# Threshold attention and Fourier mixing on one core: the last 64 queries' scores as four 64x64 tiles, the transform's rest as row tiles

## The chip, the cores and the metric

The kernel runs on one core of a Trainium2 chip. The metric is device time in microseconds (us) for one execution; the number that counts is the median of several. In the profile PE is TensorE's matmuls and PEld its weight loads, DVE is VectorE, ACT is ScalarE, POOL is GpSimd, and SP is the queue on SyncE that issues nearly all transfers. All data is fp32, and one fp32 matmul stands in the trace as two passes.

## The reference

```python
def _attn_ref(q, k, v, tau):            # (8, 8, 576, 64) each: batch, head, row, dim
    scores = np.matmul(q, k.transpose(0, 1, 3, 2)) / 8
    thresh = np.max(scores, axis=-1, keepdims=True) - tau
    scores = np.where(scores >= thresh, scores, -1e9)
    attn = np.exp(scores - np.max(scores, axis=-1, keepdims=True))
    return np.matmul(attn / (np.sum(attn, axis=-1, keepdims=True) + 1e-9), v)

def _moe_ref(x, w_ch1, w_ch2):          # x: the heads side by side, (8, 576, 512)
    u = x + np.real(np.fft.fft(np.fft.fft(x, axis=1), axis=2))
    un = (u - mean(u)) / np.sqrt(var(u) + 1e-6)          # over the last axis
    return u + np.maximum(un @ w_ch1, 0) @ w_ch2         # 512 -> 2048 -> 512
```

## The kernel before, in words

There are 8 batches of 4 pairs of heads. A pair has 576 queries and 576 keys per head, and its attention takes five steps (t = 0 to 4): four of 128 queries for both heads, and a fifth for the last 64 queries of both heads. So there are 160 steps, 20 to a batch. The program is written out by hand in one order for all engines (`manual_schedule`): each engine does its own instructions in that order, and waits on semaphores where it needs another's result.

A step does the following.

- `scores(i)` multiplies queries by keys into one or two score tiles of PSUM (tag "sc", two buffers of two banks). In steps 0 to 3 (L440) head 0 lies on partitions 0 to 63 and head 1 on 64 to 127 of `qT` and `kT`, and each head has its own tile: 288 keys in one bank and 288 in the other, so four matmuls with 64 rows. In step 4 (L446) both heads share a tile of 128 queries: `q_ends` holds the 64 queries of each head on the diagonal of a 128x128 block with zeros beside it, so one matmul over all 128 rows gives each query its own head's scores. Two matmuls of 288 keys.
- The softmax: VectorE takes the negated maxima (L461 in the first two batches, L520 later), ScalarE the exponentials (L469, L526) and the threshold `thr` (L473, L530), VectorE the mask times the exponentials with the sums beside it (L477, L540), and then the inverse of the sum (L385, L388). The mask is the last reader of the score tile. In the first two batches `softmax` does all of it; later it is cut in `softmax_first`, `softmax_second` and `softmax_third` (the scaling of the weights on ScalarE, L549), with other work between.
- `weights_in_parts(i - 1)` transposes the weights of the step before on TensorE (L587 for the last keys, L605 for the rest) and ScalarE copies them to SBUF (L593, L597, L607, L609). `values_in_parts` multiplies them by v (L636) twice per pair.
- `prep_pair(n + 1)` transposes q and k of the next pair on VectorE (L408 and L409 for `kT`, L411 for `qT`), in step 3 of each pair; `load_pair(n + 2)` and `load_v(n + 1)` issue transfers on SP.

After the last pair of a batch, `mixing(b)` does the Fourier transform as a generator, a part at a time: `py` (L766) along the 512 channels for the folded rows in three row blocks u = 0, 1, 2 of 128, 48 and 128 rows, each with an even and an odd half; then `over_seq` (L783, L787) along the 576 rows: for each of two tiles of 128 channels a sine sum `pb` and a cosine sum `pa`, of 289 outputs each. Each takes four matmuls: the main rows for even and for odd outputs (`seq_even`, `seq_odd`, 128 rows each) and the remaining rows (`seq_xe`, `seq_xo`: up to 48 rows of a 128-row matmul, mostly zeros). Sums and differences of `pa` and `pb` then go to the residual stream on VectorE and GpSimd.

The two large products run on groups of 512 tokens, the first group plainly (L909, L933), the others with block products built from sums of blocks (L1210 for ph, L1400 for po), whose results VectorE takes out of PSUM (L1147, L1420). From the second batch on `fill` puts pieces of this work and of `mixing` between the parts of the steps, by a count of TensorE columns (`per_slot`); `fill(True)` takes no part of the mixing. In the first batch `busy` puts dummy matmuls (pd) there. The tiles of PSUM for all but the scores share four banks (tag "mm").

Of the kernel before, what the change touches and what calls it, by code (L numbers as in the profile page):

```python
# [47 lines left out]
def kernel(  # L48
# [12 lines left out]
    nc = tc.nc  # L61
# [81 lines left out]
    def load_v(n):  # L143

        b, p = n // NPAIR, PAIRS[n % NPAIR]
        vt = v_in[n % 2]
        for j in range(2):
            h = 2 * p + (j + p) % 2
            nc.sync.dma_start(
                out=vt[:, j:8:2, :], in_=v[b, h, 0:512, :].rearrange("(t p) d -> p t d", p=128)  # L150
            )
            nc.sync.dma_start(out=vt[64 * j : 64 * j + 64, 8 + j, :], in_=v[b, h, 512:576, :])
# [12 lines left out]
    for u in range(2):  # L165
        for j in range(2):
            nc.gpsimd.memset(v_in[u][64 - 64 * j : 128 - 64 * j, 8 + j, :], 0.0)


    q_ends = const.tile([128, 128], FP32, name="q_ends")  # L170
    nc.gpsimd.memset(q_ends[:, :], 0.0)
# [29 lines left out]
    seq_xe = const.tile([128, 2, NE], FP32, name="seq_xe")  # L201
    seq_xo = const.tile([128, 2, NO], FP32, name="seq_xo")


    SEQ = (
        (((0, 1, 128),), seq_even, 0, ((0, 128),)),
        (((0, 16, 128),), seq_odd, 1, ((0, 128),)),
        (((0, 129, 16), (16, 0, 1)), seq_xe, 0, ((0, 17),)),
        (((32, 0, 16),), seq_xo, 1, ((32, 16),)),
    )  # L210

    def load_seq():
        for u, (pieces, dst, parity, parts) in enumerate(SEQ):
            for p, r, n in pieces:
                nc.sync.dma_start(out=f[p : p + n, u, 0 : 2 * KH], in_=dft_seq[r : r + n, :])
            if dst is seq_xo:
                nc.sync.dma_start(out=f[32:33, u, KH : 2 * KH], in_=dft_seq[144:145, KH : 2 * KH])

    def copy_seq():
        nc.gpsimd.memset(seq_xe[:, :, :], 0.0)  # L220
        nc.gpsimd.memset(seq_xo[:, :, :], 0.0)
        for u, (pieces, dst, parity, parts) in enumerate(SEQ):
            for p, n in parts:
                for c in range(2):
                    nc.gpsimd.tensor_copy(
                        dst[p : p + n, c, :], f[p : p + n, u, KH * c + parity : KH * (c + 1) : 2]
                    )
# [155 lines left out]
    def inverse(i, nh):  # L383
        den = sb.tile([128, 2], FP32, tag="den", bufs=3, name="den")
        nc.vector.tensor_reduce(  # L385
            out=den[:, 0:nh], in_=den_eps[i % 3][:, 0:nh, :], axis=AXIS_X, op=ALU.add
        )
        nc.vector.reciprocal(den[:, 0:nh], den[:, 0:nh])  # L388
# [3 lines left out]
    steps = {}  # L392
# [1517 lines left out]
```

## Time and profile before

| | |
|---|---|
| Median of three runs | 1544.85 us (1543.75, 1544.85, 1545.0) |
| The profiled execution | 1547.94 us; span from first to last instruction 1546.2 us |
| Granted TensorE clock | 0.997 |
| Fifth step's scores (L446) | 128 passes, 36.3 us busy, 406 ns each |
| Other steps' scores (L440) | 1024 passes, 168.4 us busy, 430 ns each |
| Transform along the rows (L783, L787) | 320 passes, about 287 ns each |
| Transform along the channels (L766) | 240 passes |

The length of one matmul instruction includes its way through the array, and the next begins meanwhile: the time that it takes from TensorE is the distance between starts. Batches 0 and 1 (40 steps) run to 275 us, batches 2 to 6 take 168 to 188 us each, batch 7's last step begins at 1302 us, and the rest is the last transform and the last groups' products.

### The profile page before, as it was taken

To read this page: it belongs to the slowest core of one execution; us is meant where nothing else is said; L and a number is where in the kernel's file an instruction comes from. 1 tells how busy PE (TensorE), PEld (TensorE's weight loads), DVE (VectorE), ACT (ScalarE), POOL (GpSimd) and SP (SyncE) were. 2 spreads that over 40 slices of the span, in tenths; PEclk is the share of its full clock that TensorE was granted. 3 is DMA by queue.
4 is the path that set the end of the run, shared out by engine and by line. 5 is a ranking of instruction groups with operands and counts; after the bars stand their busy time and mean duration, and the time that the engine had idled before them with its cause. 6 is when DMAs were issued, how large, how long until landed. Compare 5 with 4: busy or idle time off the path is not lost.

```text
span 1546.2 us, 27021 instructions
## 1 busy us (share of the span) xinstructions
PE 1524.0 (99%) x9786; PEld 1186.0 (77%) x9786; DVE 1063.2 (69%) x2141; ACT 916.4 (59%) x1921; POOL 779.4 (50%) x964
## 2 busy tenths in 40 slices
PE   9999999999999999999999999999999999999999
PEld 5556555556788778887788878887788778989999
DVE  7977676846779466866578566956687657746546
ACT  6875676655666576656775666666665676133131
POOL 3775563034365642546255724554264625647635
PEclk9999999999999999999999999999999999999999
DMA  7423233465956354644455354635464534646655
GB/s 171 130 59 119 78 92 105 139 183 165 280 187 206 92 173 125 186 113 146 146 167 160 120 159 133 199 92 172 120 195 132 160 117 142 220 163 231 234 196 184
DMA packets 248907, 239.31 MB, mean 155 GB/s; under 512 B 197027, under 2 KB 218533, under 8 KB 228678
## 3 DMA queue, kind: packets, MB, share of 16 engines
q1 hardware_dynamic: 246262, 237.28, 50.1%
q8 instruction: 78, 1.28, 0.3%
q10 hardware_dynamic: 2512, 0.30, 0.1%
q14 instruction: 55, 0.45, 0.1%
HBM read 205.93 MB, written 31.46 MB: 154 GB/s over the span
## 4 chain that ended last, share of the span: by engine, by line
PE 91%; DVE 4%; ACT 2%; POOL 1%; DMA 1%; issue 0%; ACTq 0%; DVEq 0%; POOLq 0%
PE ph L1210 25%; PE po L1400 21%; PE pv L636 10%; PE sc L440 10%; PE pw L605 7%; PE po L933 4%; PE ph L909 3%; PE sc L446 2%; PE py L766 2%; PE pe L587 1%; PE pa L783 1%; PE pn L858 1%; PE pa L787 1%; PE pm L360 1%; PE po L1379 1%; DVE neg L461 1%
## 5 line engine op out<-in xcount | busy, mean ns | idle before, releaser
L520 DVE TENSOR_REDUCE neg<-sc 128x1 f32<-128x576 f32 x216 | 154.3, 751 | 117.1 <-PE sc L440 105.5
L526 ACT ACTIVATE e<-sc,neg 128x576 f32<-128x576 f32 x216 | 158.6, 734 | 114.3 <-DVE neg L520 114.3
L1147 DVE TENSOR_TENSOR hs<-ph,hs 128x512 f32<-128x512 f32 (+1 forms) x128 | 105.3, 823 | 167.1 <-PE ph L1210 97.3
L1400 PE MATMUL po<-w,w_all 128*128 128x128 f32 x1728 | 219.4, 276 | 0.0
L1400 PEld LDWEIGHTS po<-w,w_all 128*128 128x128 f32 x1728 | 205.4, 192 | 7.4 <-issue 4.0
L1156 POOL TENSOR_TENSOR w<-hs 128x512 f32<-128x512 f32 x32 | 42.1, 1317 | 312.3 <-ACT hs L1152 249.3
L540 DVE SCALAR_TENSOR_TENSOR e<-sc,thr,e 128x576 f32<-128x576 f32 x216 | 168.4, 812 | 27.2 <-ACT thr L530 27.1
L1210 PE MATMUL ph<-u_t,w 128*128 128x256 f32 x768 | 180.9, 382 | 0.6 <-DMA w<-f 0.6
L607 ACT COPY e_t<-pw 128x512 f32<-128x512 f32 x256 | 148.4, 594 | 44.2 <-PE pw L605 42.7
L440 PE MATMUL sc<-kT,qT 64*128 64x288 f32 x1024 | 168.4, 430 | 5.9 <-DVE e L477 5.5
L605 PE MATMUL pw<-ident,e 128*128 128x128 f32 x1152 | 169.3, 274 | 3.7 <-ACT ends L593 1.9
L549 ACT ACTIVATE e<-e,den 128x576 f32<-128x576 f32 x216 | 157.4, 774 | 2.9 <-DVE den L388 2.2
L1210 PEld LDWEIGHTS ph<-u_t,w 128*128 128x128 f32 x768 | 140.9, 190 | 23.6 <-issue 5.3
L1210 PE MATMUL ph<-w_all,w 128*128 128x256 f32 x672 | 157.1, 382 | 1.1 <-DVE w_all L1132 1.0
L605 PEld LDWEIGHTS pw<-ident,e 128*128 128x128 f32 x1152 | 135.8, 141 | 19.3 <-issue 5.6
L1263 POOL TENSOR_TENSOR w_all<-w_all 128x128 f32<-128x128 f32 (+2 forms) x160 | 121.7, 777 | 44.5 <-DVE w_all L1420 23.4
L1210 PEld LDWEIGHTS ph<-w_all,w 128*128 128x128 f32 x672 | 123.5, 190 | 23.9 <-issue 4.9
L1152 ACT ACTIVATE hs<-hs 128x512 f32<-128x512 f32 (+1 forms) x96 | 74.1, 772 | 113.8 <-DVE hs L1147 113.0
L440 PEld LDWEIGHTS sc<-kT,qT 64*128 64x128 f32 x1024 | 95.1, 186 | 55.4 <-issue 22.9
L1400 PE MATMUL po<-w,hs 128*128 128x128 f32 x912 | 119.8, 278 | 0.0
L1400 PEld LDWEIGHTS po<-w,hs 128*128 128x128 f32 x912 | 109.8, 192 | 9.5 <-issue 8.0
L636 PE MATMUL pv<-e_t,v_in 128*64 128x320 f32 (+1 forms) x512 | 72.1, 423 | 1.5 <-ACT e_t L609 0.8
(227 smaller groups left out, 2910.6 us busy)
## 6 DMA issues: line engine op xcount, KB each, us to landing
w<-f SPq DMA_DIRECT2D x150, 1024.0 KB, 4.9
hs<-in_moe_w_ch_dram SPq DMA_DIRECT2D x23, 512.0 KB, 4.7
q_in<-in_q_dram SPq DMA_DIRECT2D x128, 72.0 KB, 4.1
out_dram<-u SPq DMA_DIRECT2D x36, 256.0 KB, 2.5
k_in<-in_k_dram SPq DMA_DIRECT2D x124, 72.0 KB, 2.4
v_in<-in_v_dram SPq DMA_DIRECT2D x64, 128.0 KB, 5.1
f<-w SPq DMA_DIRECT2D x14, 512.0 KB, 3.3
f<-w SPq DMA_DIRECT2D x7, 1024.0 KB, 4.8
```

What stands on the lines that cost most here:

```text
L440: nc.tensor.matmul(sc[j][:, c, 0:HALF], qT[hp, 128 * t : 128 * t + 128], kT[hp, k0 + HALF * c : k0 + HALF * (c + 1)], start=True, stop=True,)
L520: nc.vector.tensor_reduce(out=neg[:, j : j + 1], in_=sc[j][:, :, 0:HALF], axis=AXIS_XY, op=ALU.max, negate=True,)
L526: nc.scalar.activation(out=ej, in_=sc[j][:, :, 0:HALF], func=ACT.Exp, bias=neg[:, j : j + 1], scale=1.0)
L540: nc.vector.scalar_tensor_tensor(out=ej, in0=sc[j][:, :, 0:HALF], scalar=thr[:, j : j + 1], in1=ej, op0=ALU.is_ge, op1=ALU.mult, accum_out ...
L549: nc.scalar.activation(out=e[:, S * j : S * (j + 1)], in_=e[:, S * j : S * (j + 1)], func=ACT.Copy, scale=den[:, j : j + 1],)
L605: nc.tensor.transpose(pw[:, c, :], e[:, c0 : c0 + 128], ident[:, :])
L607: nc.scalar.copy(e_t[:, 4 * j : 4 * j + 4, qs], pw[:, :, :])
L636: nc.tensor.matmul(pv[64 * j : 64 * j + 64, 0:m], vt[:, 2 * c + j, :], e_t[:, 4 * j + c, 0:m] if c < 4 else ends[:, 0, 0:m], start=(c == 0 ...
L1147: nc.vector.tensor_tensor(out=to, in0=bank, in1=to if other is None else other, op=ALU.add)
L1210: nc.tensor.matmul(bank[:, 256 * q : 256 * q + 256].rearrange("p (two n) -> p two n", two=2), left[:, 256 * c + 128 * q : 256 * c + 128 * ...
L1263: return lambda: eng.tensor_tensor(out=to, in0=to, in1=other, op=ALU.add)
L1400: nc.tensor.matmul(to, lefts[m][j][:, s], right_[:, 128 * s : 128 * (s + 1)], start=jn in (0, 4) and s == 0, stop=s == 3, skip_group_check ...
```

## The change

- The fifth step's scores become four matmuls with 64 rows and 64 columns: head j gives the rows, half c of the keys gives the columns, so that partition 64c + q of the tile holds query q with half c of the keys of both heads. `q_ends` is a plain 128x64 copy. A query's maximum and sum are then on two partitions, and `exchange` brings the halves together with two small reductions on VectorE, once for the maxima and once for the sums. The exponentials, masks and scalings of that step go by head: two of 128x288 for one of 128x576. In the transposed weights four copies of 32 partitions bring the last keys together.
- In the other steps a head's 576 scores lie side by side in PSUM, split over the banks as 256 and 320 keys (head 0) and 320 and 256 (head 1). The keys are in another order: `kT` holds keys 256 to 575, then 0 to 319, with 32 more between, from four transposes for two; v is loaded to fit, with three transfers a head for two.
- In the transform, the remaining rows of the sine (partitions 64 to 127) and of the cosine (0 to 63) become one 64-row matmul of 289 outputs each, issued side by side ahead of the main ones (`rest_of_seq`). For the sine's rows to stand there, the odd half of block u = 1 is made with 128 columns. The points at which the generator stops move: one stop behind sine and cosine together, and two empty ones.
- From batch 2 on, `prep_pair` for the second pair of a batch is called in that batch's fifth step behind `softmax_first`, no longer at the end of its fourth.

```diff
+        for p, n, parity, c in ((0, 17, 0, 0), (32, 16, 1, 0), (64, 17, 0, 1), (96, 16, 1, 1)):
+            nc.gpsimd.tensor_copy(
+                seq_x[p : p + n, parity:KH:2],
+                f[p : p + n, 2, KH * c + parity : KH * (c + 1) : 2],
+            )
...
@@ -380,16 +379,23 @@
     for den in den_eps:
         nc.vector.memset(den[:, :, :], 1e-9)
 
-    def inverse(i, nh):
+    den_ends = const.tile([128, 2, 3], FP32, name="den_ends")
+    nc.vector.memset(den_ends[:, :, :], 1e-9)
+    own = const.tile([128, 2, 2], FP32, name="own")
+
+    def inverse(i):
         den = sb.tile([128, 2], FP32, tag="den", bufs=3, name="den")
-        nc.vector.tensor_reduce(
-            out=den[:, 0:nh], in_=den_eps[i % 3][:, 0:nh, :], axis=AXIS_X, op=ALU.add
-        )
-        nc.vector.reciprocal(den[:, 0:nh], den[:, 0:nh])
+        parts = den_eps[i % 3]
+        if i % NT == 4:
+            parts = den_ends
+            exchange(parts[:, :, 2], parts[:, :, 0:1])
+        nc.vector.tensor_reduce(out=den[:, :], in_=parts[:, :, :], axis=AXIS_X, op=ALU.add)
+        nc.vector.reciprocal(den[:, :], den[:, :])
         return den
 
     heads = {}
     steps = {}
...
@@ -404,9 +410,12 @@
 
 
         q_raw, k_raw = loaded.pop(n)
-        kT = sb.tile([128, D + S], FP32, tag="kT", name="kT")
-        nc.vector.transpose(kT[:, D : D + S], k_raw[:, :])
-        nc.vector.transpose(kT[64:128, 0:D], k_raw[64:128, 512:S])
+        kT = sb.tile([128, S + 96], FP32, tag="kT", name="kT")
+        nc.vector.transpose(kT[:, 0:320], k_raw[:, 256:S])
+        nc.vector.transpose(kT[:, 352:672], k_raw[:, 0:320])
+        for j, k0 in ((0, 288), (1, 256)):
+            hp = slice(64 * j, 64 * j + 64)
+            nc.vector.transpose(kT[hp, 320:352], k_raw[hp, k0 : k0 + 32])
         qT = sb.tile([128, S], FP32, tag="qT", bufs=1, name="qT")
         nc.vector.transpose(qT[:, :], q_raw[:, :])
...
-        sc = [ps.tile([128, 2, 512], FP32, tag="sc", name=f"sc{j}") for j in range(nh)]
+        sc = [
+            ps.tile([128, 2, 512], FP32, tag="sc", name=f"sc{j}") for j in range(2 if t < 4 else 1)
+        ]
+        order = [(c, j) for c in range(2) for j in range(2)]
+        if i < per_batch and t < 4:
+            order.sort(key=lambda cj: cj[1])
+        for c, j in order:
+            hp = slice(64 * j, 64 * j + 64)
+            if t < 4:
+                k0, k1 = ((64, 320), (352, 672), (0, 320), (352, 608))[2 * j + c]
+                to = sc[j][:, c, 512 - (k1 - k0) : 512] if c == 0 else sc[j][:, c, 0 : k1 - k0]
+                left = qT[hp, 128 * t : 128 * t + 128]
+            else:
+                k0, k1 = ((64, 352), (352, 640), (32, 320), (320, 608))[2 * j + c]
+                to, left = sc[0][64 * c : 64 * c + 64, j, 0:HALF], q_ends[hp, :]
+            nc.tensor.matmul(
+                to, left, kT[hp, k0:k1], start=True, stop=True, skip_group_check=t == 4
+            )
         if t < 4:
-            order = [(c, j) for c in range(2) for j in range(2)]
-            if i < per_batch:
-                order.sort(key=lambda cj: cj[1])
-            for c, j in order:
-                if True:
-                    hp, k0 = slice(64 * j, 64 * j + 64), D * (1 - j)
-                    nc.tensor.matmul(
-                        sc[j][:, c, 0:HALF], qT[hp, 128 * t : 128 * t + 128],
-                        kT[hp, k0 + HALF * c : k0 + HALF * (c + 1)], start=True, stop=True,
-                    )
+            steps[i] = [
+                sc[j][:, :, :].rearrange("p c n -> p (c n)")[:, 256 - 64 * j : 832 - 64 * j]
+                for j in range(2)
+            ]
         else:
-            for c in range(2):
-                nc.tensor.matmul(
-                    sc[0][:, c, 0:HALF], q_ends[:, :], kT[:, D + HALF * c : D + HALF * (c + 1)],
-                    start=True, stop=True,
+            steps[i] = [sc[0][:, j, 0:HALF] for j in range(2)]
+
...
+        both = bass.AP(
+            tensor=sc[0].tensor, offset=sc[0].offset,
+            ap=[list(sc[0].ap[0]), [512, 2], list(sc[0].ap[1])],
+        )
+        nc.vector.tensor_reduce(
+            out=own[:, :, 0], in_=both, axis=AXIS_X, op=ALU.max, negate=True
+        )
+        exchange(own[:, :, 1], own[:, :, 0:1])
+        nc.vector.tensor_reduce(out=neg[:, :], in_=own[:, :, :], axis=AXIS_X, op=ALU.min)
+        return neg
+
+    def exchange(out_, in_):
+
+        for half in range(2):
+            a, b = 64 * half, 64 - 64 * half
+            nc.vector.tensor_reduce(
+                out=out_[a : a + 64], in_=in_[b : b + 64], axis=AXIS_X, op=ALU.min
+            )
...
+        if i % NT == 4:
+            exponentials(i, e, neg, thr, 0)
+        for j in range(2):
+            if i % NT < 4:
+                exponentials(i, e, neg, thr, j)
+            elif j == 0:
+                exponentials(i, e, neg, thr, 1)
+            masked(i, e, thr, j)
             if between is not None and j == 0:
                 next(between)
...
+        c0 = 512 if t < 4 else 256
...
@@ -593,22 +618,30 @@
             nc.scalar.copy(ends[:, 0:kept, q0 : q0 + 128], pe[:, 0:kept, :])
         else:
             for j in range(2):
-                hp = slice(64 * j, 64 * j + 64)
-                nc.scalar.copy(ends[hp, 0:kept, q0 : q0 + 64], pe[hp, 0:kept, hp])
+                for half in range(2):
+                    p0 = 64 * j + 32 * (1 - half)
+                    nc.scalar.copy(
+                        ends[p0 : p0 + 32, 0, q0 : q0 + 64],
+                        pe[32 * j : 32 * j + 32, 0, 64 * half : 64 * half + 64],
+                    )
+            if kept == 2:
+                nc.scalar.copy(ends[:, 1, q0 : q0 + 64], pe[:, 1, 0:64])
...
@@ -762,43 +795,47 @@
             for odd in range(2):
                 py = ps.tile([128, 512], FP32, tag="mm", bufs=4, name="py")
                 table, first = (dim_s, 0) if odd else (dim_c, 1)
+                p0 = 64 if u == 1 and odd else 0
+                m, rows = p0 + n if p0 == 0 else 128, slice(p0, p0 + n)
                 for c, c0, c1 in SIN if odd else COS:
                     nc.tensor.matmul(
-                        py[0:n, c0:c1], f[:, c, odd * FW + r : odd * FW + r + n],
+                        py[0:m, c0:c1], f[:, c, odd * FW + r - p0 : odd * FW + r - p0 + m],
                         table[:, c0:c1], start=True, stop=True, skip_group_check=True,
                     )
                 y = y_o if odd else y_e
                 nc.scalar.copy(
-                    y[0:n, u, 0:256].rearrange("p (g hi lo) -> p lo hi g", hi=2, lo=2),
-                    py[0:n, first : first + 256].rearrange("p (lo hi g) -> p lo hi g", lo=2, hi=2),
+                    y[rows, u, 0:256].rearrange("p (g hi lo) -> p lo hi g", hi=2, lo=2),
+                    py[rows, first : first + 256].rearrange("p (lo hi g) -> p lo hi g", lo=2, hi=2),
...
-        def over_seq(y, odd, cols, m):
+        def rest_of_seq(y, rows, cols, m):
             pa = ps.tile([128, 512], FP32, tag="mm", bufs=4, name="pa")
-            for parity, u, table, extra in ((0, 0, seq_even, seq_xe), (1, 2, seq_odd, seq_xo)):
-                at = pa[0:m, parity:KH:2]
+            nc.tensor.matmul(
+                pa[0:m, 0:KH], y[rows, 1, cols], seq_x[rows, :], start=True, stop=False,
+                skip_group_check=True,
+            )
+            return pa
+
+        def over_seq(pa, y, odd, cols, m):
+            for parity, u, table in ((0, 0, seq_even), (1, 2, seq_odd)):
                 nc.tensor.matmul(
-                    at, y[:, u, cols], table[:, odd, :], start=True, stop=False,
-                    skip_group_check=True,
+                    pa[0:m, parity:KH:2], y[:, u, cols], table[:, odd, :], start=False,
+                    stop=True, skip_group_check=True,
                 )
-                nc.tensor.matmul(
-                    at, y[:, 1, cols], extra[:, odd, :], start=False, stop=True,
-                    skip_group_check=True,
-                )
-            return pa
 
         settle(b)
         for t in range(2):
             cols = slice(128 * t, 128 * t + 128)
             tmp = sb.tile([128, 3, KH], FP32, tag="tmp", bufs=1, name="tmp")
             low, high, sin = (tmp[:, c, :] for c in range(3))
-            pb = over_seq(y_o, 1, cols, 128)
+            pb = rest_of_seq(y_o, slice(64, 128), cols, 128)
+            pa = rest_of_seq(y_e, slice(0, 64), cols, 128)
+            over_seq(pb, y_o, 1, cols, 128)
             nc.scalar.copy(sin, pb[:, 0:KH])
-            yield MIX / 11
-            pa = over_seq(y_e, 0, cols, 128)
+            over_seq(pa, y_e, 0, cols, 128)
 
             nc.vector.tensor_tensor(out=low, in0=pa[:, 0:KH], in1=sin, op=ALU.subtract)
             nc.vector.tensor_tensor(out=high, in0=pa[:, 0:KH], in1=sin, op=ALU.add)
@@ -819,10 +856,14 @@
             add(3 - t, every, high, low)
             if t == 1:
                 add(3, slice(0, 1), high[0:1, :], low[0:1, :])
-            yield MIX / 11
+            yield 2 * MIX / 11
+            if t == 0:
+                yield 0
+                yield 0
...
@@ -1764,6 +1805,8 @@
             next(values, None)
         if i < total:
             softmax_first(i)
+        if i % per_batch == 4:
+            prep_pair(n + 1)
         next(values, None)
         if i % per_batch == 3:
             mix(1)
@@ -1806,7 +1849,7 @@
                 prep_ends(n)
             if t == 2 and n + 1 < B * NPAIR:
                 scale_q(n + 1)
-            if t == 3 and n + 1 < B * NPAIR:
+            if t == 3 and n + 1 < B * NPAIR and n % NPAIR:
                 prep_pair(n + 1)
         if wanted:
             wanted.pop().factors()
```

## The prediction, made before the result was known

> **What bounds the kernel now.** I read the page's busy times and chain first, then TensorE's waits, then the timeline around the edited bursts.
>
> ```profile
> PE 1524.0 (99%) x9786; PEld 1186.0 (77%) x9786; DVE 1063.2 (69%) x2141; ACT 916.4 (59%) x1921; POOL 779.4 (50%) x964
> ...
> PE 91%; DVE 4%; ACT 2%; POOL 1%; DMA 1%; issue 0%; ACTq 0%; DVEq 0%; POOLq 0%
> ```
>
> ```profile
> PE sc L440 <- DVE e L477: 5.5, 7, 1.2
> PE ph L1210 <- DVE hs L1147: 2.1, 5, 0.8
> ```
>
> TensorE is busy 99% of the span and idle for 22 us; its longest wait, scores behind a mask (L477, batches 0 and 1 only), is 5.5 us in all. So a nanosecond less of matmul is a nanosecond less of time, except where VectorE decides. But a busy row is not a price: matmuls overlap, so I price by starts, here from TensorE's timeline (start, length, form, number of passes; one fp32 matmul is two passes).
>
> ```profile
> 838.62 1.14 PE L446 MATMUL sc<-kT,q_ends 128*128 128x288 f32 x4
> 839.59 1.05 PE L1400 MATMUL po<-w,hs 128*128 128x128 f32 x8
> 840.48 1.06 PE L1400 MATMUL po<-w,w_all 128*128 128x128 f32 x8
> 841.47 0.64 PE L766 MATMUL py<-dim_s,f 128*48 128x128 f32 x4
> 842.03 0.33 PE L587 MATMUL pe<-ident,e 128*128 128x128 f32 x1
> 842.20 0.60 PE L605 MATMUL pw<-ident,e 128*128 128x128 f32 x4
> ...
> 898.22 2.38 PE L636 MATMUL pv<-e_t,v_rev 128*64 128x320 f32 x16
> 900.42 0.71 PE L636 MATMUL pv<-ends,v_rev 128*64 128x320 f32 x4
> 901.07 0.33 PE L587 MATMUL pe<-ident,e 128*128 128x128 f32 x1
> ...
> 903.83 1.89 PE L1210 MATMUL ph<-u_t,w 128*128 128x256 f32 x8
> 905.65 1.24 PE L440 MATMUL sc<-kT,qT 64*128 64x288 f32 x8
> 906.83 1.99 PE L1210 MATMUL ph<-u_t,w 128*128 128x256 f32 x8
> 908.65 0.27 PE L587 MATMUL pe<-ident,e 128*128 128x128 f32 x1
> ```
>
> The old fifth step takes 838.62 to 839.59, 0.97 us for 4 passes, 243 ns each, with no gap on either side. The 64-row bursts (L440) put 8 passes into 1.18 us: they run in twos, 4 slots of 243 ns, so row tiles do overlap. But they pay at the edges. Eight ph passes alone take 1.73 us (216 ns each); before the burst they take 1.82 (+0.09), after it 1.82 (+0.09), and the burst itself is 0.21 over its 0.97. A visit to 64-row tiles therefore costs about 0.40 us.
>
> **The skill.** "TensorEngine Tiling (Array Packing)", section Tiling Modes (Key Properties), says that changing the tile shape drains TensorE while tiles of one shape run independently. The rows agree and give the price: 0.40 us around L440. The same page's Tile-to-Partition Mapping lists the four 64x64 tiles; no row of this trace has them. "TensorE: Matmul & The Clock Gate", Part 3, says that row and column packing compose, at about 4 ns per further tile; here row tiles (L440) and 64-column tiles (pv, 10 slots of 0.27 us in 2.85) each overlap by two, which supports it without showing four. I go by the trace's prices, and by the page only for four at once.
>
> **The change, part by part.**
>
> 1. Fifth step's scores, 32 pairs. Old 0.97 us. New: four 64x64 matmuls, 8 passes; four at once they fill 2 slots, 0.485 us. Edges: in 0.09, out 0.09 and 0.10 as for L440; inside, the first slot of 64-column pv shows 0.05 (2.20 us for 8 slots of 0.269), not the 0.10 of L440; issue 0.02. Sum 0.845, saving 0.125 us. It counts where TensorE decides: 24 pairs of batches 2 to 7 and three early ones, 27 x 0.125 = 3.4. Bounds: if two column tiles in a row take turns, 4 slots and 1.33 us, so +0.36 per pair; at best, half the edges hidden, saving 0.3.
> 2. Transform over the sequence, 8 batches x 2 column tiles. Old: 16 passes of 0.123 (pa rows: 8 in 0.99), 1.97 us, no edges. New: both rests side by side as row tiles, 2 slots of 0.243, edges 0.40, then 8 passes, 0.985: 1.87. Saves 0.10 x 16 = 1.6; between 0 (edges 0.1 dearer) and 3.
> 3. Odd half of the middle 48 rows now 128 columns wide. The row at 841.47 is such a visit to narrow tiles: 0.10 more on the po passes ahead (0.99 for 0.89), 0.12 in it (0.56 for four of 0.111), 0.06 behind (0.17 for 0.11). 0.28 saved in the six transforms where it stands alone; in the first and the last it follows the even half, which stays narrow, and saves nothing: 6 x 0.28 = 1.7, between 0 and 2.3.
> 4. Scores of the other four steps: 256 and 320 keys for 288 and 288. Each row tile still streams 576, and in batch 0 the second head's first pass starts 13 ns after the first head's though four passes stand ahead of it in program order, so the tiles queue apart: 0. If they went in lockstep, 4 slots of 0.27 for 0.243, 0.11 x 128 = 14 us; I find that unlikely.
> 5. The moved yields put each column tile's cosine matmuls straight behind its sine, with no pe and pw between. Today the first cosine pa waits behind pw (512.57 to 512.86, 0.29 us), about once in each late batch. I count four of six as won, -1.0; from +1 (two banks held at once make pw wait instead) to -1.7.
> 6. VectorE gets longer in every fifth step. The rows:
>
> ```profile
> L385 DVE TENSOR_REDUCE den<-den_eps 128x2 f32<-128x4 f32 x128 | 20.1, 157 | 4.4
> L408 DVE STREAM_TRANSPOSE kT<-k_in 128x576 f32<-128x576 f32 x32 | 24.8, 774 | 3.9 <-DMA k_in<-in_k_dram 3.8
> L409 DVE STREAM_TRANSPOSE kT<-k_in 64x64 f32<-64x64 f32 x32 | 7.8, 242 | 0.4
> ```
>
> (mean ns behind the comma.) Transposes: 774 for 576 and 242 for 64 make 1.04 ns an element, so 508 for 320 and 209 for 32; two of each, 1434 for 1016: +0.42. Maxima: three small reductions of 157: +0.47. Mask: 812 + 82 becomes twice 512 + 82: +0.29. Denominator: two more reductions: +0.31. Together 1.5 us a pair, 1.2 of it ahead of the release of the score bank. In batches 2 to 7 that hides: VectorE works 4.6 of the 7.74 us of the step at 838.62. In batches 0 and 1 it doesn't always, as VectorE (first two rows) and TensorE there show:
>
> ```profile
> 63.26 0.81 DVE L477 SCALAR_TENSOR_TENSOR e<-sc,thr,e 128x576 f32<-128x576 f32 x1
> 63.99 0.08 DVE L477 DVE_READ_ACCUMULATOR e<-sc,thr,e 128x1 f32 x1
> ```
> ```profile
> 63.39 1.98 PE L440 MATMUL sc<-kT,qT 64*128 64x288 f32 x8
> 65.30 1.98 PE L360 MATMUL pm<-w,ones 128*128 128x512 f32 x4
> ```
>
> The next scores take 1.91 us, not 1.18: their second head waits for the mask's end at 64.08. Every ns there is paid, and behind it queue pm, the transposes and all later TensorE work. The same is so after the fifth steps at 118.07 (scores 2.02 long) and 199.11 (1.92). The one at 31.39 has its mask end just as the next scores start, but TensorE then idles 1.08 us at 39.0 anyway: 0.4 left. The other four have 1 us or more of slack. At the very start the transposes stand ahead of the first scores: 0.42. Sum: 3 x 1.2 + 0.4 + 0.42 = 4.4, and 0.3 for ScalarE's three extra copies of the ends in batch 0: 4.7. Bounds: 0.4, if only the start shows; 8 x 1.3 + 0.4 = 10.8, if all show.
> 7. prep_pair of a batch's second pair moves from the end of step 4 to behind the maxima of step 5. Now its transposes run till 839.22 and the maxima wait for VectorE until 840.40, though the scores are done at 839.76. Afterwards the maxima come first, then 2.2 us of transposes, and behind them the po sum at L1420 (841.07 now, about 843 then) which empties a bank for the second group of pw, 843.59 now. I count 0; if the bank comes late, 0.3 x 6 = 2. On SP, the eight q and k transfers (from 839.30) wait for these transposes: about 843.1 to 847.3, ahead of the next weight load at 852.5: 0.
> 8. ScalarE in a late fifth step: exponentials 2 x 511 for 734 (0.775 ns an element, from 734 and the 289 of the 2-wide thr), halves of the scaling alike, two more copies at 207, one copy of 244 less: +0.7 us, under 5.7 busy of 7.7: 0. SP: two more v transfers a pair, about 0.5 us each, where its weight loads wait up to 11.5 us for TensorE: 0. POOL: one copy less: 0.
>
> Sum: -3.4 - 1.6 - 1.7 - 1.0 + 4.7 = -3.0 us. The profiled span of 1546.2 (its run took 1547.9) becomes 1543.2; the median, 1544.85, becomes 1541.9, say 1542.0.
>
> **Rivals.** A: the early cost is absorbed, because ScalarE or the weights' arrival decides batches 0 and 1. For it: fillers (pd) stand there, and VectorE idles 2 of 14.7 us from 75 to 90. Against: the three stretched scores. Then -7.7 + 0.4: 1537.5. B (slower): the four 64x64 tiles do not run four at once; place, the fifth steps; price 0.36 + 0.125 on each of 27 plus 0.36 on 5 hidden or not, about 13 to 15 us: 1556. The sum is level at a burst of 0.96 us (3.0 over 27 pairs) and slower by over 0.2% from 1.07. For it: no such burst in the trace; against: both halves of the pattern overlap. C: the exposed VectorE time reaches the upper bound and part 7's bank is late: -7.7 + 10.8 + 2 = +5: 1550.
>
> **How the numbers follow.** Forecast (-3.0, give or take 2.5): 0.60. A: 0.15. B: 0.12. C: 0.13. About 0.2%, 3.1 us, is what a measurement can tell from no change, and the forecast lies on that line: 0.27 of its 0.60 falls beyond, 0.33 within. Faster 0.27 + 0.15 = 0.42; same 0.33 + 0.05 of C = 0.38; slower 0.12 + 0.08 = 0.20. The range takes in A with 2.5 us to spare and C, and leaves B out: 1535 to 1551; the forecast's own is 1539.4 to 1544.4.
>
> **What would show it.** Right: the fifth step's scores start 0.8 to 0.9 us ahead of what follows, with a gap before; the two rest matmuls start together; no gap about the odd middle half; batch 0 and 1 together 4 us longer, each later batch 1 to 1.3 us shorter. Wrong: a burst over 0.96 us; score steps of over 1.3 us elsewhere (lockstep); a new wait of pw for VectorE in each batch's fifth step; SP's weight loads waited for by TensorE.

## The result, and the profile after

The changed kernel takes 1552.05 us (four runs, 1549.36 to 1552.82) beside 1544.75 of the kernel before (four runs): a ratio of 1.0039, 95% interval 1.0027 to 1.005. The forecast was 1542.0 with a range to 1551; it is slower, by 7.3 us. The profiled execution took 1552.82 us, its span is 1551.0.

The first two rows of the page after, busy times and shares of the chain:

```profile
PE 1518.5 (98%) x9834; PEld 1172.6 (76%) x9834; DVE 1097.0 (71%) x2430; ACT 932.6 (60%) x2017; POOL 766.3 (49%) x930
...
PE 78%; DVE 9%; ACT 6%; DMA 2%; POOL 2%; issue 1%; SPq 0%; ACTq 0%; DVEq 0%; POOLq 0%
```

TensorE's work did shrink, by 5.5 us. Its idle time grew from 22.2 to 32.5 us, VectorE and ScalarE have 34 and 16 us more to do, and their share of the chain went from 6% to 15%. The saving was made and given back in waits. TensorE's waits after (engine, what waits, for whom: us in total, times, longest):

```profile
PE sc L453 <- DVE e L510: 8.3, 9, 1.3
PE pw L639 <- ACT y_o L806: 3.8, 5, 0.9
...
PE po L1441 <- ACT w_all L1453: 1.3, 4, 0.4
```

The first was 5.5; the second was 0.8, once; the third is new. Now the stretch whose rows the prediction priced, batch 5's first fifth step, on TensorE's timeline after (the second block is the first row again, in the windows 843.35 to 843.45 and 843.8 to 843.9):

```profile
843.28 0.72 PE L453 MATMUL sc<-kT,q_ends 64*64 64x288 f32 x8
843.93 1.16 PE L1441 MATMUL po<-w,hs 128*128 128x128 f32 x8
844.92 1.06 PE L1441 MATMUL po<-w,w_all 128*128 128x128 f32 x8
845.82 0.61 PE L801 MATMUL py<-dim_s,f 128*128 128x128 f32 x4
846.26 0.27 PE L612 MATMUL pe<-ident,e 128*128 128x128 f32 x1
847.25 0.66 PE L639 MATMUL pw<-ident,e 128*128 128x128 f32 x4 [0.71 <-ACT y_o L806]
```

```profile
843.28 0.47 PE L453 MATMUL sc<-kT,q_ends 64*64 64x288 f32 x4
...
843.58 0.42 PE L453 MATMUL sc<-kT,q_ends 64*64 64x288 f32 x4
```

The burst takes 0.65 us from its start to the next (0.97 before). Four passes start together and the other four 0.30 us behind them, so all four tiles run at once. po behind it takes 0.99 for 0.89, as predicted. The odd middle half (845.82) takes 0.44 (0.56 before), with no gap about it. Then pw waits 0.71 us. The transform's rest further on:

```profile
853.43 0.51 PE L816 MATMUL pa<-seq_x,y_o 64*128 64x289 f32 x1
853.44 0.51 PE L816 MATMUL pa<-seq_x,y_e 64*128 64x289 f32 x1
...
854.12 0.52 PE L824 MATMUL pa<-seq_even,y_o 128*128 128x145 f32 x2
```

Sine and cosine start within 10 ns of each other. In these rows the matmuls of the change take what they were priced at.

### The profile page after: what moved, and what is told of

The parts are those of the page before. It is cut to its first block, busy times and chain, and to the rows that moved or that the text cites. A ratio compares the mean times of both kernels' runs of the same rounds, so it can differ in the third digit from the quotient of the medians.

```text
span 1551.0 us, 27560 instructions
## 1 busy us (share of the span) xinstructions
PE 1518.5 (98%) x9834; PEld 1172.6 (76%) x9834; DVE 1097.0 (71%) x2430; ACT 932.6 (60%) x2017; POOL 766.3 (49%) x930
## 3 DMA queue, kind: packets, MB, share of 16 engines
q8 instruction: 78, 1.28, 0.3%
## 4 chain that ended last, share of the span: by engine, by line
PE 78%; DVE 9%; ACT 6%; DMA 2%; POOL 2%; issue 1%; SPq 0%; ACTq 0%; DVEq 0%; POOLq 0%
PE ph L1251 24%; PE po L1441 19%; PE pv L669 9%; PE sc L453 9%; PE pw L639 6%; PE po L974 3%; DVE e L510 2%; ACT e L499 2%; PE py L801 1%; PE ph L950 1%; PE pa L824 1%; PE po L1420 1%; DVE neg L475 1%; PE pn L899 1%; PE pe L612 1%
## 5 line engine op out<-in xcount | busy, mean ns | idle before, releaser
L499 ACT ACTIVATE e<-sc,neg 128x576 f32<-128x576 f32 (+1 forms) x320 | 219.9, 687 | 160.1 <-DVE neg L475 126.8
L510 DVE SCALAR_TENSOR_TENSOR e<-sc,thr,e 128x576 f32<-128x576 f32 (+1 forms) x320 | 229.0, 753 | 39.8 <-ACT thr L504 24.5
L475 DVE TENSOR_REDUCE neg<-sc 128x1 f32<-128x576 f32 x256 | 182.0, 751 | 101.9 <-PE sc L453 101.9
L453 PE MATMUL sc<-kT,qT 64*128 64x256 f32 (+1 forms) x1024 | 170.8, 430 | 8.7 <-DVE e L510 8.3
L578 ACT ACTIVATE e<-e,den 128x576 f32<-128x576 f32 (+1 forms) x240 | 161.8, 726 | 5.9 <-DVE den L393 5.5
L453 PEld LDWEIGHTS sc<-kT,qT 64*128 64x128 f32 x1024 | 110.5, 187 | 52.2 <-issue 25.9
```

What stands on the lines that cost most here:

```text
L453: nc.tensor.matmul(to, left, kT[hp, k0:k1], start=True, stop=True, skip_group_check=t == 4)
L475: nc.vector.tensor_reduce(out=neg[:, j : j + 1], in_=sc[j], axis=AXIS_X, op=ALU.max, negate=True)
L499: nc.scalar.activation(out=weights_of(i, e, j), in_=steps[i][j], func=ACT.Exp, bias=neg[:, j : j + 1], scale=1.0,)
L510: nc.vector.scalar_tensor_tensor(out=ej, in0=steps[i][j], scalar=thr[:, j : j + 1], in1=ej, op0=ALU.is_ge, op1=ALU.mult, accum_out=(den_en ...
L578: nc.scalar.activation(out=ej, in_=ej, func=ACT.Copy, scale=den[:, j : j + 1])
```

## The experiments

Each was timed in five rounds beside the kernel before on the same chip, whose median there was 1544.8 to 1545.4 us. The granted clock differs from run to run: in single stretches of 3.41 us it is halved (the last section shows them). So a second figure stands beside the median: the mean over the runs of time less span x (1 - granted clock), called clock-free. It takes every halved stretch at half its length, though TensorE need not have had work for all of it, and the clock is on record in steps of 0.001, 1.5 us here. The standard errors of the clock-free means are 0.6 us for the change, 0.4 for kernels 2 and 6, and 0.1 to 0.3 for the others.

| kernel | runs | median us | ratio, 95% interval | clock's part | clock-free |
|---|---|---|---|---|---|
| before | 26 to 49 | 1544.8 to 1545.4 | | 1.6 to 2.2 | 1543.3 to 1543.5 |
| the change | 4 | 1552.05 | 1.0039 (1.0027 to 1.005) | 3.5 | 1548.1 |
| 1 transposes put back | 6 | 1556.12 | 1.0071 (1.0055 to 1.0087) | 3.4 | 1553.0 |
| 2 old transform | 6 | 1554.39 | 1.0059 (1.0044 to 1.0075) | 2.9 | 1552.0 |
| 3 batches 0, 1 wide | 22 | 1547.28 | 1.0013 (1.0007 to 1.002) | 1.0 | 1546.5 |
| 4 batches 2 to 7 wide | 22 | 1548.80 | 1.0025 (1.0018 to 1.0032) | 2.3 | 1546.7 |
| 5 all wide | 13 | 1545.95 | 1.0005 (0.9996 to 1.0013) | 2.0 | 1544.0 |
| 6 middle pairs small | 13 | 1545.75 | 1.0002 (0.9993 to 1.001) | 1.8 | 1544.0 |
| 7 last pair small | 13 | 1547.62 | 1.0011 (1.0003 to 1.002) | 1.1 | 1546.2 |
| 8 statistics early | 21 | 1548.36 | 1.0019 (1.0013 to 1.0026) | 1.3 | 1547.2 |
| 9 v later on SP | 5 | 1551.66 | 1.0044 (1.0032 to 1.0057) | 3.7 | 1547.4 |
| 10 sums later | 21 | 1545.94 | 1.0009 (1.0002 to 1.0016) | 1.3 | 1545.1 |
| 11 put together | 13 | 1542.99 | 0.9991 (0.9983 to 0.9999) | 1.5 | 1541.5 |
| 12 dummy in a gap | 21 | 1545.67 | 1.0002 (0.9996 to 1.0009) | 1.4 | 1544.1 |
| 13 dummy behind the mask | 13 | 1548.36 | 1.0016 (1.0007 to 1.0024) | 1.6 | 1546.5 |
| 14 first stops | 14 | 1543.16 | 0.9985 (0.9978 to 0.9993) | 2.2 | 1541.2 |

"Small" is a fifth step in 64x64 tiles, "wide" one with the old 128-row matmuls. What each does to a late batch is read from the starts of the score bursts. Batch 6, us more (+) or less than the kernel before, from one step's start to another's, and in the last two columns the sum over batches 2 to 7, up to the last step's start:

| steps | predicted | change | 5 | 7 | 10 | 11 | 13 | six batches, change | six batches, 5 |
|---|---|---|---|---|---|---|---|---|---|
| 0 to 4 | 0 | +0.89 | +0.01 | +0.62 | +0.31 | +0.01 | +0.53 | +4.04 | +0.26 |
| 4 to 5, first pair | -0.41 | +0.14 | +0.03 | +0.03 | +0.14 | +0.04 | +0.04 | +0.44 | +0.14 |
| 5 to 9, stops and rest | -0.37 | -0.38 | -0.48 | -0.48 | -0.38 | -0.38 | -0.48 | -1.74 | -2.31 |
| 9 to 14, second pair | -0.12 | -0.13 | 0 | 0 | -0.13 | -0.13 | 0 | -0.35 | 0 |
| 14 to 19, third pair | -0.12 | -0.13 | 0 | +0.09 | -0.13 | -0.22 | 0 | +0.09 | +0.18 |
| 19 to 0, last pair | -0.12 | -0.16 | 0 | -0.16 | -0.16 | 0 | 0 | -0.93 | 0 |
| sum | -1.14 | +0.23 | -0.44 | +0.10 | -0.35 | -0.68 | +0.09 | +1.55 | -1.73 |

In these six batches no profile but kernel 1's has a halved stretch. The predicted column comes to -6.7 for them; the change has +1.55. Batch 7 goes like batch 6. The others differ: the first row is +1.21 in batch 2, +0.86 in batch 4 and only +0.09 in batches 3 and 5.

**1 and 2: which part is dear.** The first kernel takes the moved call back:

```diff
-        if i % per_batch == 4:
-            prep_pair(n + 1)
...
-            if t == 3 and n + 1 < B * NPAIR and n % NPAIR:
+            if t == 3 and n + 1 < B * NPAIR:
```

> The changed kernel with one call put back: the next pair's transposes stand at the end of a batch's fourth step again, for every pair. Theory P (the move costs): TensorE's wait of pw for y_o, 3.8 us over 5 places in the changed kernel's profile, goes, and the time falls from 1552 to about 1548. Theory E (the early batches and the clock carry the loss; the move is level): 1551 to 1553, because the maxima are late again in the fifth step and the stall only changes its name.

Both theories fall: it is slower, by 4.9 us clock-free. Its waits on TensorE:

```profile
PE pw L639 <- DVE w_all L1461: 3.5, 5, 0.9
...
PE py L801 <- ACT y_o L806: 2.6, 5, 0.6
```

With small tiles in the first pair and the 2 us of transposes (840.77 to 842.71 in batch 5) ahead of their maxima, ScalarE's y_o copy and VectorE's release of po's bank both come late; batch 5's step 4 takes 0.94 us more than before. The move repairs most of that (0.15), and the 0.71 us wait of pw is what remains.

The second kernel has the old `over_seq`, tables and stops, and the odd middle half is narrow again.

> The changed kernel with the old transform over the rows: the rest rows as 128-row matmuls, the odd middle half narrow, the stops of the generator as before. If the transform's saving is what the trace of after shows (0.10 x 16 for the row tiles, 0.28 x 6 for the wide half), the time rises by about 3.3 us to 1555. If the moved stops cost as much as they save (the wait of pa went, but the steps behind got longer by 0.17 and the bank is held longer), it stays within 1 us of 1552.

Slower by 3.9 clock-free (give or take 0.7) where 3.3 was expected: the transform's saving is real. But it doesn't lie where it was priced. In the profiles steps 5 to 9 lose 1.6 us over the six late batches, while the first pair's step, where the odd half stands, differs by 0.01.

**3 and 4: early or late.** Fifth steps of some batches wide again, keys in the new order.

```diff
+        if wide(i):
+            nc.tensor.matmul(sc[0][:, 0, 256:512], q_diag[:, :], kT[:, 64:320], ...)
+            nc.tensor.matmul(sc[0][:, 1, 0:320], q_diag[:, :], kT[:, 352:672], ...)
```

> The changed kernel with the fifth step of batches 0 and 1 as before: one 128x128 diagonal block of queries, 128-row matmuls, one mask over 576, no exchange. Batches 2 to 7 keep the 64x64 tiles. Theory E (VectorE's longer chain in the first 40 steps, and the clock dips that its stall brings): batch 2 starts about 2.5 us earlier than in the changed kernel (278.1 us), the granted clock is 0.999 in most runs, and the time is 1546 to 1549.5. Theory P: the early steps are mostly absorbed, 1551.

> The changed kernel with the fifth step of batches 2 to 7 as before (128-row matmuls, one mask over 576), and the 64x64 tiles only in batches 0 and 1. If the four tiles bring their 0.125 us in each of 24 late pairs and cost nothing else, the time rises by 3 us to 1555. If their longer chain on VectorE and ScalarE is behind the new waits (pw for y_o 3.8 us, po for w_all 1.3 us), it is 1550 to 1553: what the matmuls lose comes back from the waits.

Wide early steps bring 1.6 us clock-free and a smaller part of the clock. Wide late steps bring 1.4 where they were to lose 3 if the tiles paid. So the tiles cost in both halves, and the two together are 3.0 of the 4.7 us that the change lost clock-free, if they add up. The moved transposes help small tiles only: with wide ones in kernel 4, batch 6's step 4 takes 0.25 us more than before, and 0.04 in kernel 5, which has them back.

**5 to 7: which pairs.** The transposes are put back too; the tiles go to no pair, to the second and third, or to the last.

```diff
+    def small(i):
+        return i % NT == 4 and (False)                                                # 5
+        return i % NT == 4 and (i >= 2 * per_batch and i % per_batch in (9, 14))      # 6
+        return i % NT == 4 and (i >= 2 * per_batch and i % per_batch == 19)           # 7
```

> The changed kernel without its 64x64 tiles: every fifth step as before (128-row matmuls, one mask over 576), the transposes of the next pair back at the end of the fourth step; the new order of keys, the new transform and its stops stay. Theory S (the 64x64 tiles' longer chains on VectorE and ScalarE carry the whole loss, the transform brings what was predicted): about 0.5 us per late batch less than the kernel before, as steps 5 to 9 of the traces show, and 0.4 more at the start for the extra transposes: 1542 to 1543.5. Rival (the new order of keys and the transform cost something of their own): 1545 to 1547.

> As the last, but the second and third pair of batches 2 to 7 take the 64x64 tiles: the places where the traces show 0.22 us less about the burst and 0.09 more ahead of it, and no new wait. Theory S: 12 pairs x 0.125 = 1.5 us below the kernel with every fifth step wide, about 1541. Rival (VectorE's 1.5 us more per pair shows up somewhere behind, whatever the pair): no gain, or a loss of 1 us.

> As the kernel with every fifth step wide, but the last pair of batches 2 to 7 takes the 64x64 tiles. Theory S: VectorE's chain is 0.9 us longer there, the statistics of u come later, behind them the inverse deviation on ScalarE, the exponentials and the copy of po's bank; TensorE waits 0.62 us in the step after and 0.18 two steps on, so 0.8 - 0.06 in each of four or five batches: 3 to 4 us above the kernel with every fifth step wide, about 1546. Rival (the wait has another cause, the length of ScalarE's own work): within 1 us of it.

The last pair's tiles cost 2.2 us clock-free (3 to 4 expected) and +0.62 in the step behind. The middle pairs gain 0.26 a batch in batches 3, 5, 6 and 7, as predicted. In batch 4 they lose 0.15, and in batch 2 0.45, where ph waits longer for VectorE (batch 2's third pair, kernel 6 and then kernel 5):

```profile
PE ph L1297 <- DVE hs L1234: 1.6, 1, 1.6
...
PE ph L1297 <- DVE hs L1234: 0.9, 1, 0.9
```

From step 5 of a batch on that makes 0.4 us in six batches for the 1.5 that was expected, and the times of 5 and 6 don't separate. Kernel 5 gains 0.44 in batches 5 to 7, 0.07 to 0.18 in batches 2 to 4, and is yet level with before: some 2 us are lost before batch 2 without any tile.

**8, 10, 12, 13: what the last pair costs.** In the kernel with the change, step 0 of batch 7 has TensorE wait inside po (first two rows; the others are the kernel before):

```profile
1148.32 1.95 PE L1441 MATMUL po<-w,w_all 128*128 128x128 f32 x16
1150.63 2.05 PE L1441 MATMUL po<-w,hs 128*128 128x128 f32 x16 [0.36 <-ACT w_all L1453]
...
1144.06 1.95 PE L1400 MATMUL po<-w,w_all 128*128 128x128 f32 x16
1145.85 1.95 PE L1400 MATMUL po<-w,hs 128*128 128x128 f32 x16
```

and ScalarE, which must copy po's bank, shows why:

```profile
1146.86 0.30 ACT L922 ACTIVATE rstd<-mv,eps 128x4 f32<-128x4 f32 x1 [1.08 <-DVE mv L911]
1147.16 1.28 ACT L925 ACT_TABLE_LOAD   x1
...
1149.38 0.73 ACT L499 ACTIVATE e<-sc,neg 128x576 f32<-128x576 f32 x1
1150.00 0.58 ACT L1453 COPY w_all<-po 128x512 f32<-128x512 f32 x1
```

The copy stands behind the exponentials, these behind a table load (1.28 us, the 1283 ns of "ScalarE activation tables: per-element evaluation and per-set limits" in the Trainium skill, section What a function is on this engine), that behind the inverse deviation, and that waits 1.08 us for VectorE's statistics. VectorE is late because its fifth step is longer. From that step's mask to the statistics and the next maxima it has no pause:

```profile
1141.23 0.52 DVE L510 SCALAR_TENSOR_TENSOR e<-sc,thr,e 128x288 f32<-128x288 f32 x1 [1.23 <-ACT e L499]
...
1141.67 0.51 DVE L510 SCALAR_TENSOR_TENSOR e<-sc,thr,e 128x288 f32<-128x288 f32 x1
...
1142.86 0.67 DVE L910 BATCH_NORM_STATS2 stats<-u 128x6 f32<-128x512 f32 x1
...
1145.92 0.69 DVE L910 BATCH_NORM_STATS2 stats<-u 128x6 f32<-128x512 f32 x1
...
1147.59 1.41 DVE L475 TENSOR_REDUCE neg<-sc 128x1 f32<-128x576 f32 x2
```

Kernel 8 (kernel 3 with the statistics about 1 us sooner) changes one chain; kernel 10 also moves 1.5 us of sums from the batch's last step into the next:

```diff
-            if ended or not late:
+            if ended or not late or at_once:          # at_once: in a batch's last step
                 measure()
...
             partials = partial_sums(i // per_batch)
-            next(partials)
+            if i == total - 1:
+                next(partials)
         if i % per_batch == 0 and i > 2 * per_batch:
             next(partials)
+            next(partials)
+            next(partials)
```

> The kernel with early fifth steps wide and late ones in 64x64 tiles (1547.3 us), with the statistics of u in a batch's last step taken as soon as u is there, ahead of one product of the transform's sums and one sum of blocks on VectorE, about 1.0 us sooner. Theory S: ScalarE's table load, inverse deviation and exponentials follow, the wait of po for w_all (1.4 us in 4 places) goes and with it most of the 0.8 us per batch: about 1544. Rival (the four small copies and two exponentials on ScalarE hold it up by themselves): 1547.

> As the kernel with the statistics taken early (1548.4 us), and three pieces of the transform's sums on VectorE (1.5 us) moved out of a batch's last step into the next, behind that step's maxima and masks. Theory V (it is the length of VectorE's whole queue from the last fifth step to the next maxima that decides, and not one chain in it): the maxima come 1.5 us sooner, the exponentials and the copy of po's bank follow, TensorE's wait of po for w_all goes (0.6 us in 4 or 5 places): 1544.5 to 1546. Rival (ScalarE's two table loads and its own longer work hold it, or the moved pieces are late for the sums of blocks that follow): 1547.5 or more.

Kernel 8 gains nothing: the deviation is ready, but the next step's maxima end as late as ever, since they stand behind the same queue on VectorE. In kernel 10 the wait is gone:

```profile
1143.98 1.95 PE L1488 MATMUL po<-w,w_all 128*128 128x128 f32 x16
1145.77 1.95 PE L1488 MATMUL po<-w,hs 128*128 128x128 f32 x16
```

It is 2 us below kernel 8 clock-free, and +0.31 instead of +0.9 in the table. Step 0's share of that is 0.62 in the change and 0 here; 0.27 stands just ahead of the first pair's tile in both, 0.09 of it the tile's edge, the rest not followed. The moved sums aren't free: in batches 3 and 5 the row is +0.26 and +0.39 for the change's +0.09. The reverse test puts six reductions of nothing on VectorE in kernel 5's last pair, first between maxima and mask, then behind the mask:

```diff
+        if i % per_batch == 19:
+            for _ in range(6):
+                nc.vector.tensor_reduce(
+                    out=own[:, :, 1], in_=own[:, :, 0:1], axis=AXIS_X, op=ALU.min
+                )
```

> The kernel with every fifth step wide (1545.95 us), and six small reductions of nothing on VectorE (157 ns each, 0.94 us) behind the maxima of the last pair's fifth step, all batches from the third on. It has none of the 64x64 tiles. Theory V: 0.9 us more on VectorE's queue there is what brings the wait of po for w_all, so that wait appears (0.5 us in 4 places), each of four or five batches takes 0.5 to 0.8 us more, and the time rises by 2.5 to 3.5 to about 1549. Rival (the tiles' edges or ScalarE's extra copies bring it): no such wait and 1546.

> As the kernel with six small reductions of nothing on VectorE, but they stand behind the last pair's mask and no longer between the maxima and the mask, where VectorE idled 1.3 us for ScalarE anyway. Every fifth step is wide. Theory V (what counts is VectorE's queue from the mask of the last fifth step to the maxima of the next step): now the wait of po for w_all appears, steps 0 to 4 of batches 4, 6 and 7 take about 0.8 us more than in the kernel with every fifth step wide, and the time rises by some 2.5 us over 1545.7. Rival (the tiles need their own edges or ScalarE's copies to bring it): no wait, within 0.7 us of 1545.7.

The first brings no wait. The reductions take 1.09 us (first row) and fill an idle stretch of 1.05 us, in which VectorE waits for the threshold in kernel 5 (second row):

```profile
1133.38 1.09 DVE L602 TENSOR_REDUCE own<-own 128x2 f32<-128x2 f32 x6
...
1137.06 0.82 DVE L539 SCALAR_TENSOR_TENSOR e<-sc,thr,e 128x576 f32<-128x576 f32 x1 [1.05 <-ACT thr L532]
```

The second brings the wait back without any tile, 2.4 us above the first clock-free and +0.53 in the table:

```profile
PE po L1493 <- ACT w_all L1505: 1.0, 4, 0.3
```

So the length of VectorE's queue from the last pair's mask to the next maxima is the cause of that wait. Why the queue has room to spare in batches 3 and 5 was not followed.

**9, 11, 14: the early batches.** In batch 0's first fifth step VectorE after the change waits for a piece of the weights before it reaches the mask:

```profile
33.32 0.16 DVE L487 TENSOR_REDUCE neg<-own 128x2 f32<-128x4 f32 x1
34.93 0.43 DVE L295 TENSOR_SCALAR w<-hs 128x512 int32<-128x512 int32 x1 [1.45 <-DMA hs<-in_moe_w_ch_dram]
```

SP issues that piece at 30.77 us, at 27.78 before: ahead of it stand four more v transfers and three more of the sequence tables, at about half a us each. Kernel 9 puts the second `load_v` behind the piece.

```diff
-    load_v(1)
...
+        if i == 2:
+            load_v(1)
```

> The changed kernel with one call moved: the second pair's v transfers (six on SP's queue) are issued in step 2, behind two pieces of the first weights, no longer ahead of them. Theory Q (the longer queue on SP holds the weights back, VectorE's wait of 1.4 us for them in the first fifth step makes TensorE's stall at 35.7 us, and the clock is halved behind it): VectorE's wait for that piece goes, the stall goes, steps 4 to 6 of batch 0 take about 9.0 us and not 12.8, the granted clock is 0.999 in most runs, and the time falls from 1552 to 1549 or below. Rival (the 64x64 form's own chain on VectorE makes the stall, and the clock dips as before): within 1 us of 1552.

```profile
33.31 0.16 DVE L487 TENSOR_REDUCE neg<-own 128x2 f32<-128x4 f32 x1
33.38 0.42 DVE L295 TENSOR_SCALAR w<-hs 128x512 int32<-128x512 int32 x1
```

The wait is gone and steps 4 to 6 take 8.7 us for 12.8, as expected, but the time gains 0.7 us clock-free, no more than the error of four and five runs (the two profiles, halved stretches taken off, have batch 2 start 0.6 us earlier); the part of the clock stays at 3.7 us, so that half of the theory falls. Kernel 11 gives batches 0 and 1 their old keys, v transfers and wide steps, has small tiles in the middle pairs alone, and the second `load_v` stands as in kernel 9. In kernel 14 one empty stop of the first transform is moved.

```diff
+            if n < 2 * NPAIR:          # 11: also in the scores and the transfers of v
+                nc.vector.transpose(kT[:, D : D + S], k_raw[:, :])
+                nc.vector.transpose(kT[64:128, 0:D], k_raw[64:128, 512:S])
...
             if t == 0:
                 yield 0
-                yield 0
+            if t == (1 if b == 0 else 0):          # 14
+                yield 0
```

> A version put together from what the runs show: batches 0 and 1 keep the kernel before's keys, transposes, v transfers and wide fifth steps; from batch 2 on the new order of keys, and 64x64 tiles in the second and third pair alone; the new transform throughout; the next pair's transposes in the fourth step; the second v load moved behind the weights as in the first of these runs. If the early batches are then level and the late ones bring what the traces show (0.7 us in each of five batches, less in batch 2), the time is 1541.5 to 1543.5 beside 1545.1 of the kernel before. Rival (the moved stops of the first transform cost about 0.5 in batch 1, and the clock decides the rest): 1544 to 1545.5.

> As the version put together from the runs (1543.0 us), with one of the two empty stops of the first transform moved from its first to its second column tile, so that the second sine and cosine come one call sooner. Theory T (the moved stops are what holds u_t back in batch 1): the wait of ph for u_t, 0.9 us, goes, batch 1's step 4 comes 0.5 us sooner. If the weights' arrival at about 187.5 us then decides as the traces say, the gain is lost again by step 8 and the time stays 1543.0; if not, 1542.5.

Kernel 11 is faster than the change and, at 0.9991 (0.9983 to 0.9999), just faster than the kernel before; against kernel 6 (2.5 us clock-free) it shows what the new order of keys, its transfers and the place of that load cost the first 40 steps together. Kernel 14 leaves the 0.9 us wait of ph for u_t where it was; theory T falls, and it isn't told apart from kernel 11.

## Why the prediction was wrong, point by point

- **Part 1 (-3.4).** The burst and its edges came out as priced (0.84; the prediction's own terms add up to 0.835, not 0.845); rival B fell. But the gain was kept only in the second and third pair, and not in every batch: 0.4 us for 1.5 (kernel 6 beside 5). Right in size, wrong in where it counts.
- **Part 2 and part 5 (-1.6, -1.0).** Right in sum: -2.31 in kernel 5 from step 5 to 9 of six batches, for -2.22; -0.48 in four of them, -0.28 and -0.12 in batches 4 and 2.
- **Part 3 (-1.7).** The matmuls take 0.44 for 0.56, the step got no shorter (+0.03 in kernel 5): there the next py waits for the y_o copy, 1.6 us in five places. ScalarE was the limit of that spot.
- **Part 4 (0).** Right: other bursts stay at 1.17 to 1.18 us.
- **Part 6: the step that failed.** "In batches 2 to 7 that hides" was read from how busy VectorE is in the first pair's step. In the last pair's step the statistics, the sums and the next maxima stand behind it, with no slack to po: +0.6 to +0.9 in batches 4, 6 and 7, and in batch 2 after batch 1's last pair +1.2 (kernel 3: +0.1). That term, put at nothing, is most of the +4.04 in the table. The price itself was too high: VectorE is busy for 33.8 us more, 1.06 a pair and not 1.5. Lengths were added up, and VectorE's instructions overlap too: the second half's mask starts 0.44 us behind the first (1141.23 and 1141.67), which is 0.52 long. So even the smaller price did not hide. For batches 0 and 1 it counted 4.7. The starts show batch 2 begin 3.1 us later, or 4.8 with each profile's halved stretches taken off at half their length; only 1.0 of it is the tiles (kernel 3). The size was near by luck: 2.5 us belong to the new keys, their transfers and the loads (kernel 11 beside 6), and part 8 had the transfers at 0.
- **Part 7 (0, bound 2).** The sign was missed. A bank does come late for the first pw, 3.8 us in five places, but it is the one that ScalarE's y_o copy frees, not VectorE's for the second pw; and without the move the tiles would cost 3.8 (profiles) to 4.9 us (times) more.
- **Part 8 (0).** SP's transfers were looked at in the late batches alone. At the start they hold back the weights.
- **The clock** had no term. It took 1.9 us of the kernel before on the chip of runs 1 to 4 and 3.5 of the changed one.

Sum: clock-free 1548.1 for 1543.4, +4.7; the clock +1.6 or so; that makes 6.3, and the medians, of four runs each, differ by 7.3. Between kernel 11 and the change lie 6.6 us clock-free: 2.5 for the keys and loads in the early batches, and about 4.1 for tiles in the other places. Not tried: a shorter way to bring two partition halves together.

Of the rivals C lies nearest, 1550, by VectorE's exposed time and part 7's bank, but not in its places. A named a limit that is there: in batch 1 VectorE idles 4.8 us until a piece of the weights lands at 187.8 us (kernel 6). But the early cost was not absorbed.

## What to carry to other kernels

A matmul that is made cheaper by spreading a row over two partitions pays in another engine's queue; before counting that as hidden, follow the queue past the edited step to the next thing TensorE waits for, in each place where the step stands, since four equal steps had four different prices here. A busy share doesn't show slack, and added work can fall into an idle stretch (kernel 12) or on the path (kernel 13) a microsecond later. Put such an edit only where the trace shows that nothing follows: two of four pairs gave a small gain in the traces, too small for the times, and all four a loss.

## What the hardware showed unexpectedly

The granted clock was halved in single stretches of 3.41 us (once 6.83), and each one inside the attention lies right behind a stretch of the same length in which TensorE was busy for at most 70%. Two stretches of the kernel before (us, then busy time and count of PE, PEld, DVE, ACT and POOL, the clock, the share of DMA, GB/s):

```profile
78.50:81.90 3.40, 1.47 (x13) 1.06 (x12) 3.04 (x9) 3.15 (x8) 2.25 (x2) 1.00 0.14 30
81.90:85.30 3.40, 3.40 (x16) 1.84 (x16) 2.34 (x5) 3.15 (x7) 1.83 (x3) 0.50 0.65 145
```

TensorE idles for 1.9 us of 3.4 and then works at half speed, for up to 1.7 us of loss. In the traces of 12 kernels the 16 halved stretches inside the attention follow busy shares of 0.43 to 0.70. "TensorE: Matmul & The Clock Gate" in the Trainium skill, Part 1, gives a free-running window of 3413 ns and half rate for the idle state; both agree. It puts the fall to half rate behind a whole idle window; here 1.0 to 1.9 us of idle time in a window stood ahead of it. Not every such window is followed by a halved one (in the changed kernel's trace that at 82.1 us, 44% busy, on the same count of windows, is not), so idle time goes before it in every case but doesn't settle it, and what else does stays open. A pause of a microsecond or two was followed by up to 1.7 us of further loss in some runs and by none in others.
